# Attention with decay and a squared-ReLU layer on one core: maxima sent as rows of 32, whole heads loaded ahead and rounded on VectorE, bulk loads on another queue, the clamp on GpSimd

## The chip, the cores and the metric

The kernel runs on one core of a Trainium2 chip. A core has TensorE (PE; its weight loads are shown as PEld), VectorE (DVE), ScalarE (ACT), GpSimd (POOL) and SyncE (SP), which here only issues DMA transfers. The metric is the device time of one execution in microseconds (us), lower is better. "Granted clock" is the share of full speed at which TensorE was allowed to run.

## What is computed

Attention with a learned decay over 64 heads (8 batches of 8 heads, S = 576 tokens, D = 64), and behind it a layer of two products with a squared ReLU, all in fp32 accuracy:

```python
scores = scale * q @ k.T                                # per head, 576 x 576
cum    = cumsum(log(clip(f, 1e-4, 1)))                  # per head, 576
scores = where(causal, -1e9, scores + cum[:, None] - cum[None, :])
scores = scores - max(scores, -1)                       # the row maxima
attn   = exp(scores); attn /= sum(attn, -1) + 1e-9
x      = (attn @ v), heads side by side                 # 4608 x 512
out    = relu(x @ w_in) ** 2 @ w_out                    # 512 -> 2048 -> 512
```

## The kernel before

**Heads.** Each head is worked in 6 units (the slots of the program); unit u of head h is slot 6h+u. A unit multiplies a tile of keys with a range of queries into a PSUM bank (`score`), ACT takes the exponential (L370), and two slots later the result is multiplied with v (`av_part`). The decay and the row maxima are not added by another instruction: they are additional rows under q and k, so that the same product contains them. Row D+2 of the q plane holds minus the maximum of each query's row, so no unit of a head can begin before that row is complete.

**Maxima.** While head h-1 is worked, TensorE computes rounded scores of head h (`max_units`, L320), DVE reduces each of 6 pieces (L326) to a column `tcol` of 128 (or 64) partitions, one column for each of 5 query tiles. As soon as a column is complete, SP sends it by DMA into row D+2 of the q plane (L332), five transfers a head.

**Two kinds of heads.** Heads 0 to 13 are "whole": the scores are fp32 products of the unrounded planes `rl` (L353), for which q and k are loaded twice, once rounded on the way (`load_rounded`, a DMA on POOL's queue into `rk`, L261) for the maxima and once as they are (`load_whole`, on SP's queue). Two buffers each. Heads 14 to 63 are split into rounded and remainder parts (L360, L363, L396 to L398).

**Weights.** The 32 weight arrays of 512 KB (`w0` to `w31`, 16 each of w_in and w_out) are loaded on SP's queue and split into a rounded and a remainder part by `weight_ops`, a generator that yields five times per weight: the clamp of the magnitudes (DVE, L201); the shift (DVE, L206) with the absolute value of the next weight (ACT, L190); two combining operations (DVE, L211 and L213; behind the second the next loads are issued, four weights ahead); the rounding (ACT, L218) with the subtraction (POOL, L219). `RATES` says how many yields are taken per slot: 1 up to slot -7, 2 in slots -6 to -1, 1.2 in slots 0 to 47, 2.5 from there. The layer behind the attention (`mlp1`, L483, and `mlp2`, L506) fills TensorE from slot 60 on, when the first batch's attention is finished; from then on half-steps of it are spread over the slots.

**Order.** TensorE, ACT, DVE and POOL execute in the order in which the program is traced. SP's order is set by a scheduler. The transfers that SP and ACT issue share 8 completion semaphores (DMAHW0 to DMAHW7) in turn; before a transfer is issued, its issuing queue waits until the earlier one with that semaphore has landed. SP and POOL issue all transfers of the kernel before.

## Time and profile before

| what | value |
|---|---|
| median of 3 executions | 1244.87 us (1244.57 to 1246.03) |
| the profiled execution | 1246.64 us |
| its span, first to last instruction | 1244.9 us |
| mean granted clock | 0.980 |
| TensorE busy | 1184.0 us (95%) |
| DVE, ACT, POOL busy | 787.3, 702.7, 372.1 us |
| all DMA | 71.91 MB, 58 GB/s on average |

The span is cut into stages below: the start (up to the first units), the whole heads, the beginning of the layer, and the long stretch from 300 us in which TensorE works almost without a break. Busy shares over the whole span say little of the first two stages.

### The profile page before, as it was taken

What the parts mean: (1) busy time and instruction counts of PE and PEld (TensorE: products, weight loads), DVE (VectorE), ACT (ScalarE), POOL (GpSimd) and SP (SyncE); (2) the same over time, 40 slices, a digit from 0 to 9 for tenths busy, and PEclk for the clock granted to TensorE, in tenths of its full rate; (3) what the DMA queues carried; (4) which work ended last, traced back from release to release, by engine and by line L of the source; (5) the groups of instructions that cost most, each with busy time, mean ns of one, the idle gap of its engine ahead of it and who ended that gap; (6) DMA issues with size and microseconds to landing.
All of it is one profiled execution on the core that took longest, in us unless ns stands there. A gap on an engine that the chain in (4) does not pass through costs nothing. (4 is left out here: it accounts for less than half of the span.)

```text
span 1244.9 us, 23235 instructions
## 1 busy us (share of the span) xinstructions
PE 1184.0 (95%) x7652; PEld 1045.4 (84%) x7652; DVE 787.3 (63%) x2044; ACT 702.7 (56%) x1720; POOL 372.1 (30%) x564
## 2 busy tenths in 40 slices
PE   3887899999999999999999999999999999999998
PEld 1554677888999899999999989998998899999997
DVE  6667777666677667666656666667666767533332
ACT  3564454665666666665565556766666666632332
POOL 3233323333333333332322233334333333200000
PEclk9888799999999999999999999999999999999999
DMA  8776641112121212121212121212121222000000
GB/s 186 170 164 162 161 124 27 42 41 57 37 53 36 48 41 58 41 58 26 52 22 53 31 53 35 54 35 55 41 58 41 57 41 53 16 28 1 18 18 17
DMA packets 115640, 71.91 MB, mean 58 GB/s; under 512 B 97384, under 2 KB 97384, under 8 KB 115520
## 3 DMA queue, kind: packets, MB, share of 16 engines
q1 hardware_dynamic: 114400, 66.30, 21.9%
q0 software_dynamic: 1120, 4.13, 1.6%
q8 instruction: 61, 1.00, 0.3%
q14 instruction: 59, 0.48, 0.1%
HBM read 60.20 MB, written 9.88 MB: 56 GB/s over the span
## 5 line engine op out<-in xcount | busy, mean ns | idle before, releaser
L506 PE MATMUL bank<-w,gh 128*128 128x512 f32 x1152 | 413.2, 399 | 0.0
L483 PE MATMUL bank<-xh,w 128*128 128x256 f32 x2304 | 330.0, 286 | 3.5 <-DVE tcol L326 3.4
L386 DVE TENSOR_TENSOR pl<-p,ph 128x320 fp32r<-128x320 f32 (+4 forms) x300 | 187.7, 626 | 199.4 <-ACT ph L385 195.1
L483 PEld LDWEIGHTS bank<-xh,w 128*128 128x128 f32 x2304 | 302.0, 190 | 11.5 <-DVE tcol L326 4.0
L506 PEld LDWEIGHTS bank<-w,gh 128*128 128x128 f32 x1152 | 217.1, 188 | 38.4
L506 PE MATMUL bank<-w,gl 128*128 128x512 f32 x576 | 226.8, 394 | 0.1
L491 ACT ACTIVATE r<-bank 128x256 f32<-128x256 f32 x288 | 110.6, 384 | 205.5 <-PE bank L483 180.5
L492 DVE TENSOR_TENSOR g<-r 128x256 f32<-128x256 f32 x288 | 126.3, 439 | 140.6 <-ACT r L491 139.8
L372 POOL TENSOR_SCALAR_AFFINE_SELECT p<-p 128x128 f32<-128x128 f32 (+1 forms) x250 | 80.9, 324 | 440.3 <-ACT p L370 335.5
L385 ACT CAST ph<-p 128x320 fp32r<-128x320 f32 (+4 forms) x300 | 124.4, 415 | 148.3 <-POOL p L372 105.9
L483 PE MATMUL bank<-xl,w 128*128 128x256 f32 x1152 | 185.0, 283 | 0.0
L326 DVE CUSTOM_DVE_ANT_0 bank<-bank,mz 128x256 f32<-128x256 f32 (+4 forms) x320 | 133.7, 433 | 47.8 <-PE bank L320 43.0
L483 PEld LDWEIGHTS bank<-xl,w 128*128 128x128 f32 x1152 | 158.7, 191 | 0.0
L370 ACT ACTIVATE p<-bank 128x320 f32<-128x320 f32 (+4 forms) x300 | 116.2, 388 | 65.5 <-PE bank L363 54.2
L494 DVE TENSOR_TENSOR gl<-g,gh 128x256 fp32r<-128x256 f32 x288 | 128.3, 446 | 35.4 <-PE bank L506 0.5
L320 PE MATMUL bank<-rk 66*128 66x320 f32 (+4 forms) x384 | 114.9, 328 | 25.8 <-DMA rk<-qkraw 16.1
L493 ACT ACTIVATE gh<-r 128x256 fp32r<-128x256 f32 x288 | 120.5, 418 | 9.1
L506 PEld LDWEIGHTS bank<-w,gl 128*128 128x128 f32 x576 | 109.0, 189 | 14.2 <-DVE gl L494 0.9
L320 PEld LDWEIGHTS bank<-rk 66*128 66x128 f32 (+1 forms) x384 | 70.5, 190 | 43.4 <-issue 18.6
L396 PE MATMUL bank<-pl,vh 128*65 128x320 f32 (+4 forms) x350 | 97.2, 278 | 2.2 <-ACT den L432 2.2
L397 PE MATMUL bank<-ph,v 128*64 128x320 f32 (+4 forms) x350 | 94.9, 271 | 0.0
L398 PE MATMUL bank<-ph,vh 128*65 128x320 f32 (+4 forms) x350 | 93.6, 273 | 0.0
(76 smaller groups left out, 1512.9 us busy)
## 6 DMA issues: line engine op xcount, KB each, us to landing
qkraw<-in_qk SPq DMA_DIRECT2D x50, 288.0 KB
v<-in_v SPq DMA_DIRECT2D x64, 160.0 KB
den<-rdr SPq DMA_DIRECT2D x64, 144.0 KB
out<-osb SPq DMA_DIRECT2D x36, 256.0 KB
w<-in_w_in SPq DMA_DIRECT2D x16, 512.0 KB
w<-in_w_out SPq DMA_DIRECT2D x16, 512.0 KB
rl<-in_qk SPq DMA_DIRECT2D x14, 288.0 KB
rk<-in_qk POOLq DMA_DIRECT2D x14, 288.0 KB, 4.9
```

Of the source, the lines that this page charges most:

```text
L320: nc.tensor.matmul(ps[:m, :n], st["r2"][:D + 2, q0:q0 + m], st["kl0"][:D + 2, k0:k0 + n], start=True, stop=True,)
L326: nc.vector.tensor_tensor_reduce(out=ps[:m, :n], in0=ps[:m, :n], in1=mz[:m, mo:mo + n], op0=ALU.add, op1=ALU.min, scale=-1.0, scalar=init, ...
L370: nc.scalar.activation(out=p[:kn, :n], in_=ps[:kn, :n], func=AF.Exp, scale=SCALE)
L385: nc.scalar.copy(out=ph[:kn, :n], in_=p[:kn, :n])
L386: nc.vector.tensor_tensor(out=pl[:kn, :n], in0=p[:kn, :n], in1=ph[:kn, :n].bitcast(F32), op=ALU.subtract,)
L396: nc.tensor.matmul(acc[:D + 1, o], vh, pl[:kn, i], start=first, stop=False)
L483: nc.tensor.matmul(ph[:, :T], w[:, s, cc], x[:, cc, :], start=(cc == 0 and k == 0), stop=(cc == NCC - 1 and k == 2),)
L491: nc.scalar.activation(out=r, in_=ph[:, :T], func=AF.Relu)
L492: nc.vector.tensor_tensor(out=g, in0=r, in1=r, op=ALU.mult)
L493: nc.scalar.activation(out=gh, in_=r, func=AF.Square)
L494: nc.vector.tensor_tensor(out=gl, in0=g, in1=gh.bitcast(F32), op=ALU.subtract)
L506: nc.tensor.matmul(po, g[:, ts], w[:, s], start=(fc == 0 and k == 0), stop=(fc == NF - 1 and k == 2),)
```

## The change

- The columns of maxima stay on chip until a head's last one is there. `tcol` is cleared first; one DVE transpose of 32x32 blocks turns it into `row`, where a partition holds 32 maxima of a query tile; six transfers on SP's queue (four of 4x32 elements, two of 32) write row D+2. `row` has one buffer.
- The rounding DMA on POOL's queue is gone. Each whole head is loaded once, into one of three buffers (the third shares the memory of `qkraw`), two to three heads ahead, and two DVE copies a head (`round_whole`) make the rounded planes for the maxima.
- The weights, the v of the whole heads and the q/k of whole heads from head 2 on are issued by ACT's queue and no longer by SP's.
- The clamp of the magnitudes is on POOL.
- `RATES` is (0, 2, 1.4, 2.5). With it only w0's load is issued ahead of slot -6.
- 52 products of a zero tile are put ahead of and between the maxima of head 0 (`spin`); nobody reads their bank.

```diff
     whole = [planes(wk, F32, "rl") for _ in range(2)]
+    NWB = 3
...
+    def third_whole():
+        whole.append(planes(wk, F32, "qkraw"))
+        constant_rows(nc.gpsimd, whole[2])
...
-                nc.sync.dma_start(out=raw, in_=(w_in, w_out)[i % 2][i // 2].bitcast(I32))
+                nc.scalar.dma_start(out=raw, in_=(w_in, w_out)[i % 2][i // 2].bitcast(I32))
...
         stage()
+        yield
         stage()
-        yield
         magnitude(0)
         yield
...
-            nc.vector.tensor_scalar(mag, mag, MAG_LOW, MAG_HIGH, ALU.max, ALU.min)
+            nc.gpsimd.tensor_scalar(mag, mag, MAG_LOW, MAG_HIGH, ALU.max, ALU.min)
...
-    def load_rounded(h):
+    def load_whole(h):
         x = rounded[h % 2]
-        state[h] = dict(r2=x.q, kl0=x.k, p={})
-        nc.gpsimd.dma_start(out=x.raw[:D], in_=qk[h])
+        state[h] = dict(r2=x.q, kl0=x.k, whole=whole[h % NWB], p={})
+        x = state[h]["whole"]
+        (nc.scalar if h > 1 else nc.sync).dma_start(out=x.raw[:D], in_=qk[h])
         if cum:
             load_cum(h, x.k)
-    def load_whole(h):
-        x = state[h]["whole"] = whole[h % 2]
-        nc.sync.dma_start(out=x.raw[:D], in_=qk[h])
+    def round_whole(h):
+        x, r = state[h]["whole"], rounded[h % 2]
+        nc.vector.tensor_copy(out=r.q[:D], in_=x.q[:D])
+        nc.vector.tensor_copy(out=r.k[:D, :S], in_=x.k[:D, :S])
         if cum:
-            load_cum(h, x.k)
+            load_cum(h, r.k)
...
-            nc.sync.dma_start(out=vr[:, :, :D], in_=v[h])
+            (nc.scalar if h < NWHOLE else nc.sync).dma_start(out=vr[:, :, :D], in_=v[h])
...
         tcol = wk.tile([P, 8], F32, name="tcol")
+        nc.vector.memset(tcol, 0.0)
...
-            if last:
+            if i == 0:
                 r = st["whole"].q if h < NWHOLE else st["r2"].bitcast(F32)
-                nc.sync.dma_start(out=r[D + 2:D + 3, q0:end], in_=acc)
+                row = wk.tile([P, 32], F32, name="row", bufs=1)
+                nc.vector.transpose(
+                    out=row.rearrange("p (a c) -> p a c", c=8),
+                    in_=tcol.rearrange("p (a c) -> p a c", a=1).broadcast_to([P, 4, 8]),
+                )
+                for b in range(P // 32):
+                    nc.sync.dma_start(
+                        out=r[D + 2:D + 3, D + b * 32:D + NI * P].rearrange("o (c x) -> o c x", x=32)[:, ::P // 32],
+                        in_=row[b * 32 + 1:b * 32 + 1 + NI],
+                    )
+                for b in range(D // 32):
+                    nc.sync.dma_start(out=r[D + 2:D + 3, b * 32:(b + 1) * 32], in_=row[b * 32:b * 32 + 1])
...
-    RATES = (1, 2, 1.2, 2.5)
+    RATES = (0, 2, 1.4, 2.5)
...
-                at((h - 3) * NU + 3, 0, load_rounded, h)
-                at((h - 2) * NU + 5, 1, load_whole, h)
+            if h > 2:
+                at((h - 3) * NU + 5, 1, load_whole, h)
+            if h > 1:
+                at((h - 2) * NU + 3, 0, round_whole, h)
...
+    spun = psum.tile([P, 512], F32, name="bank7")
+    def spin(n):
+        for _ in range(n):
+            nc.tensor.matmul(spun[:, :MW], mz[:, :P], mz, start=True, stop=True)
+    for i, x in enumerate(MAXIMA[False]):
+        at(int(x) - NU, int(2 * x) % 2, spin, 2 if i < 5 else 14)
+    spin(28)
     load_f()
-    load_rounded(0)
+    load_whole(0)
     convert(1)
-    load_whole(0)
     decay()
...
-    load_rounded(1)
     load_whole(1)
+    round_whole(1)
+    third_whole()
+    load_whole(2)
```

The order of the instructions moves with it, on three engines. In the rows below `w0` to `w6` are the weights, `wmag` the magnitudes, `osb` the combined words, `ph` and `pl` the exponentials; what stands in brackets are the semaphores that an instruction waits for (DMAHW: a transfer's, with the name of an engine: that engine's).

ACT before, from the first magnitude to the first exponential of head 0:

```order
L190 ACTIVATE wmag_129<-w0_100 128x512 [waits DMAHW1_49]
L190 ACTIVATE wmag_134<-w1_102 128x512 [waits DMAHW2_49,DVE_49]
L218 CAST w0_144<-osb_132 128x512 [waits DVE_49,Activation_49]
L190 ACTIVATE wmag_158<-w2_138 128x512 [waits DMAHW4_49,DVE_49]
L218 CAST w1_176<-osb_156 128x512 [waits DVE_49,Activation_49]
L190 ACTIVATE wmag_191<-w3_140 128x512 [waits DMAHW6_49,DVE_49]
L218 CAST w2_197<-osb_189 128x512 [waits DVE_49,Activation_49]
L190 ACTIVATE wmag_203<-w4_142 128x512 [waits DMAHW7_49,DVE_49]
L370 ACTIVATE ph_207<-bank1_205 128x320 [waits PE_49]
```

The same piece of ACT's order in the changed kernel (`qkraw` is the third buffer, here for head 2):

```order
L269 DMA qkraw_158<-in_qk 64x1152 [waits DMAHW4_49,DMAHW5_49,DMAHW3_49,DMAHW6_49,DMAHW2_49,DMAHW7_49,DMAHW0_49,DVE_49]
L187 DMA w1_172<-in_w_out 128x1024
L196 ACTIVATE wmag_189<-w1_172 128x512 [waits DMAHW5_49,DVE_49]
L187 DMA w2_203<-in_w_in 128x1024
L187 DMA w3_205<-in_w_out 128x1024 [waits DMAHW1_49]
L187 DMA w4_207<-in_w_in 128x1024
L284 DMA v_209<-in_v 128x5x64 [waits DMAHW1_49]
L224 CAST w0_237<-osb_187 128x512 [waits DVE_49,Activation_49]
L196 ACTIVATE wmag_243<-w2_203 128x512 [waits DMAHW7_49,DVE_49]
L187 DMA w5_247<-in_w_out 128x1024 [waits DMAHW2_49]
L224 CAST w1_249<-osb_241 128x512 [waits DVE_49,Activation_49]
L391 ACTIVATE ph_255<-bank1_253 128x320 [waits PE_49]
```

The loads now stand in ACT's own row of work: one magnitude and two roundings stand behind the loads of w2 to w4 and v, and the first exponential behind all of them. DMAHW1 in the row of v is the semaphore of w3.

POOL in the changed kernel, the first weights:

```order
L207 TENSOR_SCALAR wmag_174<-wmag_174 128x512 [waits Activation_49,Pool_49]
L286 MEMSET v_209 128x5x2
L225 TENSOR_TENSOR w0_237<-osb_187,w0_237 128x512 [waits Activation_49]
L207 TENSOR_SCALAR wmag_189<-wmag_189 128x512 [waits Pool_49]
L225 TENSOR_TENSOR w1_249<-osb_241,w1_249 128x512 [waits DMAHW5_49,Activation_49]
L207 TENSOR_SCALAR wmag_243<-wmag_243 128x512 [waits Pool_49]
L286 MEMSET v_294 128x5x2
L225 TENSOR_TENSOR w2_308<-osb_265,w2_308 128x512 [waits DMAHW7_49,Activation_49]
```

Before, POOL had only the subtractions (L219) here, with the rounding loads between them. Now the clamp of the next weight stands behind the subtraction of this one.

SP around the maxima of a split head, before:

```order
L447 DMA rdr_4229<-cmp_4148 128x9 [waits DMAHW7_49,DMAHW2_49,DVE_49]
L246 DMA qkraw_4278<-in_qk 64x1152 [waits DMAHW3_49,Activation_49,Pool_49]
L332 DMA rk_1_77<-tcol_4163 1x128x1 [waits DMAHW4_49,DVE_49]
L332 DMA rk_1_77<-tcol_4163 1x128x1 [waits DMAHW5_49,DVE_49]
L450 DMA den_3852<-rdr_4229 64x576 [waits DMAHW6_49,DMAHW2_49]
L332 DMA rk_1_77<-tcol_4163 1x64x1 [waits DVE_49]
L450 DMA den_3852<-rdr_4229 64x576 [waits DMAHW0_49]
L255 DMA rk_0_76<-cum_dr_82 2x576 [waits DMAHW1_49,PE_49]
```

and in the changed kernel:

```order
L468 DMA rdr_4879<-cmp_4799 128x9 [waits DMAHW6_49,DMAHW5_49,DVE_49]
L253 DMA qkraw_4933<-in_qk 64x1152 [waits DMAHW7_49,Activation_49,Pool_49]
L471 DMA den_4511<-rdr_4879 64x576 [waits DMAHW6_49,DMAHW0_49]
L471 DMA den_4511<-rdr_4879 64x576 [waits DMAHW1_49]
L348 DMA rk_1_77<-row_4925 1x4x32 [waits DMAHW2_49,DVE_49]
L348 DMA rk_1_77<-row_4925 1x4x32 [waits DMAHW3_49]
L348 DMA rk_1_77<-row_4925 1x4x32 [waits DMAHW4_49]
L348 DMA rk_1_77<-row_4925 1x4x32
L353 DMA rk_1_77<-row_4925 1x16x2
L353 DMA rk_1_77<-row_4925 1x16x2 [waits DMAHW7_49]
L262 DMA rk_0_76<-cum_dr_82 2x576 [waits DMAHW0_49,PE_49]
```

Single columns stood between the two transfers of `den` (the reciprocal row sums of the heads before); now all six rows stand behind both.

More of the change, by code (lines that the diff above doesn't have):

```diff
@@ L116, in planes @@
     def planes(pool, dtype, name):
[L117 removed]
+        return Planes(pool.tile([P, S + SK], dtype, name=name, **(dict(bufs=1) if name == "qkraw" else {})))
     rounded = [planes(cpool, F32R, f"rk_{i}") for i in range(2)]
     whole = [planes(wk, F32, "rl") for _ in range(2)]
+    NWB = 3
     vhs = [cpool.tile([P, NJ, D + 2], F32R, name=f"vh_{i}") for i in range(2)]
@@ L146, in decay @@
         ft, zt, ct = (fr[:NH, i, :] for i in range(3))
+        constant_rows(nc.vector, rounded[0])
         nc.vector.memset(zt, 0.0)
-        constant_rows(nc.vector, rounded[0])
         nc.vector.tensor_scalar(ft, ft, 1e-4, 1.0, ALU.max, ALU.min)
@@ L153, in decay @@
         nc.scalar.activation(out=warm_exp[:, :1], in_=warm_exp[:, :1], func=AF.Exp)
+        round_whole(0)
         nc.vector.tensor_tensor_scan(ct, zt, ft, 0.0, ALU.add, ALU.add)
@@ L239, in decay_attention_relu2_kernel @@
     NU = len(UNITS)
+    NI = len(QT) - 1
     state = {}
@@ L438, in finish @@
         if part == 0:
-            st["cmp"] = wk.tile([P, S // D], F32, name="cmp")
+            st["cmp"] = wk.tile([P, S // D], F32, name="cmp", bufs=1)
             for i in range(2):
```

1 line of the change is left out of this document (removed).

## The prediction

> **What bounds the kernel now.** I read first where the time is, in the page's slices and in a table by stage, then in the stages that are not full what TensorE waits for.
>
> ```profile
> PE   3887899999999999999999999999999999999998
> PEclk9888799999999999999999999999999999999999
> 0.00:34.00 34.00, 12.34 (x40) 7.95 (x41) 22.42 (x54) 11.92 (x20) 12.78 (x32) 1.00 0.84 188
> 34.00:131.00 97.00, 76.58 (x331) 49.12 (x330) 65.49 (x177) 51.59 (x120) 31.20 (x37) 0.82 0.70 164
> 131.00:300.00 169.00, 157.50 (x980) 134.87 (x979) 120.50 (x281) 93.09 (x227) 53.39 (x66) 0.96 0.28 72
> 300.00:1075.00 775.00, 771.28 (x5243) 703.19 (x5243) 522.35 (x1405) 489.23 (x1214) 271.80 (x424) 1.00 0.19 45
> ```
>
> The last four rows give a stretch, its length, then the busy time of PE, PEld, DVE, ACT and POOL, the granted clock, the DMA share and GB/s. From 300 us on PE is busy in 771 of 775 us at full clock: the change removes no product there, so it can only lose there. What can be gained lies ahead of 131 us, in the whole heads, where PE is busy 79% of the time at a granted 0.82. There the first unit of each head waits for its row of maxima:
>
> ```profile
> PE bank L353 <- DMA rl<-tcol: 9.3, 5, 2.9
> 24.71 0.87 PE L353 MATMUL bank<-rl 67*128 67x320 f32 x1 [4.32 <-DMA w<-in_w_out]
> 33.40 0.49 PE L353 MATMUL bank<-rl 67*128 67x320 f32 x1
> 42.24 0.51 PE L353 MATMUL bank<-rl 67*128 67x320 f32 x1 [1.18 <-DMA rl<-tcol]
> 49.54 0.28 PE L417 MATMUL bank<-pl,v 66*65 66x64 f32 x2
> 52.58 0.87 PE L353 MATMUL bank<-rl 67*128 67x320 f32 x1 [2.76 <-DMA rl<-tcol]
> 63.81 0.49 PE L353 MATMUL bank<-rl 67*128 67x320 f32 x1
> 106.23 0.87 PE L353 MATMUL bank<-rl 67*128 67x320 f32 x1 [4.71 <-issue]
> 117.76 0.51 PE L353 MATMUL bank<-rl 67*128 67x320 f32 x1
> 131.20 0.85 PE L353 MATMUL bank<-rl 67*128 67x320 f32 x1
> ```
>
> These are the first products of heads 0, 1, 2, 3, 4, 8, 9 and 10 (49.54: the last of head 2). Head 2 takes 7.6 us of PE (42.24 to 49.82) at full speed; head 3, begun behind an idle time of 2.76 us with a product of 0.87 us in place of 0.51, takes 11.2. Heads 1 to 7 take 72.8 us, 10.4 each; heads 8 and 9 take 11.5 and 13.4. All that follows is counted from these starts, since the layer begins with head 10 and fills PE from there.
>
> **The start of head 0: +9.** Today ACT has the loads of nobody in its order, and the first exponential comes 0.18 us after the product:
>
> ```profile
> 26.15 0.44 ACT L370 ACTIVATE ph<-bank 128x320 f32<-128x320 f32 x1 [0.18 <-PE bank L353]
> 16.80 0.32 SPq L255 DMA_DIRECT2D rk<-cum_dr  x1
> 11.50 1.26 POOL L219 TENSOR_TENSOR w<-osb,w 128x512 fp32r<-128x512 f32 x1 [3.78 <-issue]
> 10.74 0.62 ACT L218 CAST w<-osb 128x512 fp32r<-128x512 f32 x1 [0.83 <-DVE osb L213]
> 8.78 0.43 DVE L206 TENSOR_SCALAR osb<-wmag 128x512 int32<-128x512 int32 x1
> 9.96 0.69 DVE L213 SCALAR_TENSOR_TENSOR osb<-w,osb 128x512 int32<-128x512 int32 x1
> 2.31 0.57 POOL L132 MEMSET rl<- 32x576 f32 x1
> ```
>
> In the change ACT first issues head 2's q/k into the memory that held the cumulated sums, so it waits until those are stored; they are first read back at 16.80, which I take. Then w1 goes out, about 17.4. At 188 GB/s (first stage) 288 and 512 KB need 1.6 and 2.8 us: w1 is there at about 21.5, its magnitude follows, and w2 to w4 go out by 23. The load of v waits for the semaphore of w3, which is 5.6 us of transfers later, about 28. Behind it stand w0's rounding (0.62, 28.9) and, by way of POOL's subtraction (1.26) and the clamp of w1, DVE's shift (0.43) and two combinations (0.69 each), the rounding of w1 (0.62). No row shows the clamp on POOL; it lies between POOL's memset (0.57, one operand fewer) and its subtraction of two operands (1.26). I take the middle, 0.95. That gives 31.1, 32.9, 33.5 and the first exponential at about 34, 8 us later than now. PE fills its three banks at 25 and then waits, so it begins anew at half speed, as head 3 shows: about 1 us more. Bounds: -5, if fewer bytes let the first product come earlier than 24.71 (it waited 4.32 us) and nothing of the above binds, to +12.
>
> Of the zero products, which run in PE's idle time ahead of 24.71, nothing is left after so long a wait: 0. The Trainium skill ("TensorE: Matmul & The Clock Gate", Part 1, "What's actually happening") has an idle window of about 3.4 us after which the clock falls again; head 3's 2.76 us on this trace were enough already.
>
> **Heads 1 to 7: -7.** Three chains compete with the 7.6 us of PE. First the row of maxima:
>
> ```profile
> 47.95 0.14 DVE L326 DVE_READ_ACCUMULATOR2_ANT tcol<- 64x1 f32 x1
> 67.90 1.19 SPq L442 DMA_DIRECT2D cmp<-den  x2
> 70.48 0.18 DVE L444 TENSOR_SCALAR cmp<-cmp 128x9 f32<-128x9 f32 x1 [0.26 <-DMA cmp<-den]
> 17.23 0.23 SPq L255 DMA_DIRECT2D rl<-cum_dr  x1
> 340.16 0.39 SPq L255 DMA_DIRECT2D rk<-cum_dr  x1
> 338.84 0.59 SPq L332 DMA_DIRECT2D rk<-tcol  x1
> ```
>
> The last maximum of head 3 is read 5.85 us after head 2's start (48.09) and PE gets its row 4.5 us later. Now come a transpose (0.2, from the small operation at 70.48), four issues, and the landing of the last (from 69.09 to 70.4: 1.3). An issue of few pieces took 0.23 to 0.39 (L255, two rows), one of 128 pieces 0.59 (L332); the rows have four pieces, so 0.36 each, 1.45 in all. Sum 2.95, so a head takes at least 8.8; with other transfers in the way up to the present 4.5, 10.4.
>
> Second, the weights. Today the clamp on DVE does not wait for POOL. In the change clamp, shift, two combinations, rounding and subtraction of a weight follow each other, and the next clamp stands behind the subtraction on POOL: 0.95 + 0.43 + 0.69 + 0.69 + 0.62 + 1.26 = 4.64, and five handovers of about 0.1: 5.1 a weight. At 1.4 yields a slot a head has 1.68 weights: 8.6 us. Third, DVE and ACT lose the clamps and gain two roundings of 64x576 a head; 65 and 52 of 97 us leave room. I take 9.4, between the row's 8.8 and the 10.4 of now: 7 times -1.0. Bounds: 7.6 (-19.6) to 10.9 (+3.5).
>
> **Heads 8 and 9: +5.** At 2.5 yields a slot there are three weights a head. Now they follow at 3.5 us:
>
> ```profile
> 118.93 1.48 POOL L219 TENSOR_TENSOR w<-osb,w 128x512 fp32r<-128x512 f32 x1 [2.02 <-ACT w L218]
> 122.46 1.27 POOL L219 TENSOR_TENSOR w<-osb,w 128x512 fp32r<-128x512 f32 x1 [2.06 <-ACT w L218]
> 127.49 1.26 POOL L219 TENSOR_TENSOR w<-osb,w 128x512 fp32r<-128x512 f32 x1 [3.76 <-ACT w L218]
> 127.60 1.48 DVE L206 TENSOR_SCALAR osb<-wmag 128x512 int32<-128x512 int32 x1
> ```
>
> With 5.1 each they need 15.3 a head, against 11.5 and 13.4: +5.7; some of it can run over into head 10, so +5. Bounds -3 to +8. The shift of 1.48 us at 127.60 in place of 0.43 shows DVE slowed while POOL subtracts. The Trainium skill ("SBUF — State Buffer", section "SBUF: two separate sides") has a port pair shared by POOL and DVE, which one of them holds for a whole instruction while the other is blocked; this row agrees. By that rule the clamp on POOL, in place of one on DVE, stops DVE more often, for up to 0.95 us each time: with 1.68 clamps a head and seven heads at most 11 us, if DVE had no room.
>
> **Heads 10 to 18: 0.** They have 19 to 25 us each and 93% of PE; the clamps of the last 10 weights find room. Bounds -4 to +4.
>
> **Split heads: +6.** Here the row has no gain to make, only a margin to lose:
>
> ```profile
> 337.92 0.13 DVE L326 DVE_READ_ACCUMULATOR2_ANT tcol<- 64x1 f32 x1
> 341.72 0.31 PE L360 MATMUL bank<-rk 67*128 67x320 f32 x1
> 422.32 0.13 DVE L326 DVE_READ_ACCUMULATOR2_ANT tcol<- 64x1 f32 x1
> 424.37 0.31 PE L360 MATMUL bank<-rk 67*128 67x320 f32 x1
> 338.24 0.55 SPq L450 DMA_DIRECT2D den<-rdr  x1
> ```
>
> From the last maximum to the head's first product there are 3.67 us in most heads, and 1.92 in the shortest; in about ten of fifty (heads 18, 22, 26, 30, 42, 46 and so on) it is 1.8 to 3.1, 2.4 on average. The row needs 2.95, so these ten wait 0.55 each. The two `den` transfers (0.55 each) that now stand ahead of the rows cost nothing as long as they go before the last maximum; the columns that held them up are gone. If they do not, 1.1 us are added in every second head. Bounds 0 to +45 (issues of 0.59 and `den` in front).
>
> **The sum.** 9 - 7 + 5 + 0 + 6 = +13 on the profiled 1246.64 gives 1259.6. That execution lies 1.8 above the median of the runs, so I forecast **1258**. By bounds alone it could go from -32 to +73.
>
> **Rivals.** *Faster:* ACT's queue does not hold the start, because its transfers land sooner and the clamp is near 0.57, and the heads come down to the row's chain with a fast landing: start +2, heads 1 to 7 at 8.4 (-14), heads 8 and 9 -2: about 1231. For it speaks that PE is idle for 20 of the 97 us of the whole heads, at a granted 0.82, and that each whole head's q/k is loaded once instead of twice, at a DMA share of 0.84 and 0.70; against it the order of ACT, in which a wait for a transfer stops roundings and exponentials. The Trainium skill ("DMA: Bandwidth & Descriptors", section "Issuing engines are not separate DMA queues") holds that another issuing queue brings no bandwidth, only issue time; by it the move to ACT has nothing to give but the time of SP, and this rival rests on the saved bytes alone. *No change:* start and heads 8 and 9 (+14) are made good by heads 1 to 7 near 8.6 (-13): 1245 to 1247. *Rows late everywhere, slower by more:* issues take 0.5 and the `den` pair goes first: 0.2 + 2.0 + 1.3 + 1.1 = 4.6 against 3.67 in every second head, about 25 x 0.9, and 1.1 in ten others, 33 in all; with the +7 of the early stage 1285, or 1269 if it holds in half of them. It decides from an issue of 0.54 on without `den`, of 0.27 with both in front.
>
> **How the numbers follow.** My forecast 0.42, with its own range 1248 to 1270; faster 0.30; no change 0.12; rows late 0.16. Within 0.2% (2.5 us) is what a measurement of this kernel cannot tell from no change: 0.12; faster 0.30; slower 0.58. The range for 8 in 10 takes in the faster rival's 1231 and most of the late rows: 1229 to 1278.
>
> **What would show it.** Right: first exponential near 34, head 1 near 42; heads 1 to 7 at 9 to 10 us; subtractions of weights 5 us apart in heads 8 and 9 with POOL's clamp between them near 0.95; a PE wait on the row DMA in about ten split heads. Wrong: a first exponential before 29, a head 8 that begins before 100, or a wait on the rows in more than half of the split heads.

## The result: 6.7% slower

The changed kernel takes 1328.43 us (median of 4 executions, 1326.14 to 1331.02); the kernel before, timed beside it, 1245.45 us. The ratio is 1.0666 (95% interval 1.0641 to 1.0692): +83 us where +13 was forecast, and outside the range.

The table by stage, cut at the first products of heads 1, 10, 18 and 63. First the kernel before (columns as in the prediction: stretch, length, busy time of PE, PEld, DVE, ACT and POOL, granted clock, DMA share, GB/s):

```profile
0.00:33.40 33.40, 11.73 (x38) 7.55 (x38) 21.86 (x53) 11.32 (x19) 12.78 (x32) 1.00 0.84 189
33.40:131.20 97.80, 77.38 (x337) 49.70 (x335) 66.26 (x178) 52.19 (x121) 31.27 (x37) 0.82 0.70 165
131.20:292.53 161.33, 150.18 (x928) 128.14 (x927) 115.57 (x269) 86.29 (x211) 51.32 (x62) 0.96 0.29 74
292.53:1073.81 781.28, 777.20 (x5285) 708.55 (x5284) 525.88 (x1416) 494.92 (x1229) 272.74 (x427) 1.00 0.19 45
```

The changed kernel:

```profile
0.00:44.23 44.23, 26.89 (x90) 13.17 (x90) 18.14 (x53) 9.50 (x16) 18.42 (x35) 0.73 0.41 121
44.23:176.68 132.45, 101.42 (x335) 63.41 (x335) 67.07 (x204) 53.33 (x123) 60.21 (x48) 0.63 0.39 109
176.68:351.23 174.55, 154.31 (x926) 129.08 (x926) 116.07 (x279) 87.48 (x213) 69.63 (x72) 0.94 0.22 59
351.23:1157.27 806.04, 783.97 (x5283) 705.80 (x5284) 540.16 (x1504) 495.09 (x1226) 270.66 (x427) 1.00 0.17 43
```

Every stage is longer: +10.8 up to head 1, +34.7 in heads 1 to 9, +13.2 in heads 10 to 17, +24.8 in heads 18 to 62, together the 83.4 us between the spans (1244.9 and 1328.3). From the first product of head 63 on, both take 171 us. The DMA share fell from 0.70 to 0.39 in heads 1 to 9, as each of them is loaded once, and that bought nothing. The granted clock there fell from 0.82 to 0.63, and TensorE's busy time rose from 77.4 to 101.4 us with the same products (337 and 335 records): 24 of the 34.7 us are slower products, 10.6 are more idle time.

TensorE's waits name two things, the rows of maxima and the maxima themselves (line, what it waited for: us in total, times, longest):

```profile
PE bank L381 <- DMA rk<-row: 23.7, 29, 2.3
PE bank L330 <- DVE tcol L336: 17.9, 14, 5.2
PE bank L374 <- DMA rl<-row: 17.8, 6, 3.9
PE bank L504 <- DVE tcol L336: 6.3, 1, 6.3
PE bank L374 <- DMA qkraw<-row: 6.3, 2, 3.5
```

**The rows.** In the time lines of DVE, SP, ACT and PE around the last maximum before head 3, and around one split head, head 25:

```profile
67.31 0.13 DVE L336 DVE_READ_ACCUMULATOR2_ANT tcol<- 64x1 f32 x1
67.48 0.21 DVE L343 STREAM_TRANSPOSE row<-tcol 128x32 f32<-128x32 f32 x1
67.72 0.65 SPq L348 DMA_DIRECT2D rl<-row  x1
68.45 0.52 SPq L463 DMA_DIRECT2D cmp<-den  x1
69.03 1.89 SPq L348 DMA_DIRECT2D rl<-row  x3
69.45 0.34 ACTq L187 DMA_DIRECT2D w<-in_w_in  x1
73.63 0.87 PE L374 MATMUL bank<-rl 67*128 67x320 f32 x1 [3.73 <-DMA rl<-row]
...
465.19 0.14 DVE L336 DVE_READ_ACCUMULATOR2_ANT tcol<- 64x1 f32 x1
465.60 2.57 SPq L348 DMA_DIRECT2D rk<-row  x4
468.21 1.18 SPq L353 DMA_DIRECT2D rk<-row  x2
469.34 0.39 PE L381 MATMUL bank<-rk 67*128 67x320 f32 x1 [0.19 <-DMA rk<-row]
```

A head's first product reads queries 256 to 575 and so needs four of the six transfers. In the split head these four issues take 2.57 us, 0.64 each, and the product begins 1.2 us after the last of them: 4.0 us from the last maximum, a little over the usual margin of 3.67. Before head 3 the same work takes 6.2 us. A transfer of the row sums (L463) stands between the first row and the others, and the product comes 2.7 us after the fourth; a weight's load (512 KB) was issued by ACT meanwhile, at 69.45. TensorE stands for 3.73 us and begins again at half clock (0.87 us for a product in place of 0.51).

**The clamp.** The groups of instructions of the changed kernel for clamp, subtraction and shift (busy time, mean ns of one; idle time of the engine before them and what ended it):

```profile
L207 POOL TENSOR_SCALAR wmag<-wmag 128x512 f32<-128x512 f32 x32 | 62.8, 1963 | 0.7 <-ACT wmag L196 0.7
L225 POOL TENSOR_TENSOR w<-osb,w 128x512 fp32r<-128x512 f32 x32 | 41.6, 1300 | 130.3 <-ACT w L224 116.4 <-DMA w<-in_w_in 7.9 <-DMA rl<-in_qk 6.0
L212 DVE TENSOR_SCALAR osb<-wmag 128x512 int32<-128x512 int32 x32 | 19.1, 597 | 65.2 <-POOL wmag L207 49.1 <-POOL v L286 16.1
```

The shift in the kernel before:

```profile
L206 DVE TENSOR_SCALAR osb<-wmag 128x512 int32<-128x512 int32 x32 | 22.5, 704 | 2.5
```

The clamp takes 1.96 us on POOL, twice the estimate. DVE stands idle for 65 us ahead of its 32 shifts, waiting for POOL (49 us for the clamp, 16 for the small fill of `v` that stands behind some of the clamps); in the kernel before the same group had 2.5 us. Since DVE works in the traced order, the maxima stand behind the shift and wait with it.

### The profile page after: what moved, and what is told of

Its sections match the earlier page's. It is cut to its first block, busy times and chain, and to the rows that moved or that the text cites. A ratio compares the mean times of both kernels' runs of the same rounds, so it can differ in the third digit from the quotient of the medians.

```text
span 1328.3 us, 23358 instructions
## 1 busy us (share of the span) xinstructions
PE 1234.0 (93%) x7704; PEld 1062.9 (80%) x7704; DVE 798.4 (60%) x2168; ACT 703.1 (53%) x1720; POOL 422.1 (32%) x586
## 4 chain that ended last, share of the span: by engine, by line
PE 47%; DVE 4%; DMA 4%; SPq 4%; issue 2%; ACT 1%; POOL 0%; DVEq 0%; ACTq 0%; POOLq 0%
PE bank L504 19%; PE bank L527 17%; SPq L348 4%; DMA rk<-row 3%; PE bank L417 2%; PE bank L381 2%; PE bank L330 2%; PE bank L419 2%; PE bank L418 2%; PE bank L384 1%; DVE g L513 1%; DVE pl L407 1%; DVE bank L336 1%; ACT r L512 1%; DVE gl L515 1%
## 5 line engine op out<-in xcount | busy, mean ns | idle before, releaser
L407 DVE TENSOR_TENSOR pl<-p,ph 128x320 fp32r<-128x320 f32 (+4 forms) x300 | 196.7, 656 | 214.3 <-ACT ph L406 205.3
L513 DVE TENSOR_TENSOR g<-r 128x256 f32<-128x256 f32 x288 | 136.3, 473 | 139.3 <-ACT r L512 138.8
L330 PE MATMUL bank<-rk 66*128 66x320 f32 (+4 forms) x384 | 121.9, 347 | 21.3 <-DVE tcol L336 17.9
L381 PE MATMUL bank<-rk 67*128 67x320 f32 (+4 forms) x300 | 89.6, 299 | 24.8 <-DMA rk<-row 23.7
L330 PEld LDWEIGHTS bank<-rk 66*128 66x128 f32 (+1 forms) x384 | 74.1, 199 | 42.5 <-DVE tcol L336 26.9
```

The lines of the kernel that those rows point to most:

```text
L330: nc.tensor.matmul(ps[:m, :n], st["r2"][:D + 2, q0:q0 + m], st["kl0"][:D + 2, k0:k0 + n], start=True, stop=True,)
L407: nc.vector.tensor_tensor(out=pl[:kn, :n], in0=p[:kn, :n], in1=ph[:kn, :n].bitcast(F32), op=ALU.subtract,)
L513: nc.vector.tensor_tensor(out=g, in0=r, in1=r, op=ALU.mult)
```

## The experiments

Three theories: the rows make the loss (1), the clamp behind the subtraction on POOL does (2), the loads in ACT's order do (3). Each run is the changed kernel or the kernel before with one edit, and then with several. The results first, by stage; the first column of lengths ends at the first product of head 1. The ratio is taken against the kernel before as timed on the same chip. The lengths are those of one profiled execution each, which lies within 1.6 us of its kernel's median, with two exceptions here: "all three undone" was profiled 4.1 us above its median, and "the same, loads by ACT" 7.0 us below.

| kernel | to head 1 | heads 1-9 | heads 10-17 | heads 18-62 | median us | ratio to before (95%) |
|---|---|---|---|---|---|---|
| before | 33.4 | 97.8 | 161.3 | 781.3 | 1245.45 | |
| changed | 44.2 | 132.5 | 174.6 | 806.0 | 1328.43 | 1.0666 (1.0641-1.0692) |
| changed, columns | 39.7 | 121.5 | 174.2 | 779.4 | 1286.34 | 1.0330 (1.0291-1.0369) |
| changed, clamp on DVE | 36.5 | 121.2 | 163.6 | 808.9 | 1301.47 | 1.0452 (1.0411-1.0492) |
| changed, loads by SP | 39.1 | 122.3 | 174.1 | 809.5 | 1318.33 | 1.0587 (1.0556-1.0618) |
| changed, more zero products | 46.5 | 119.1 | 176.2 | 805.8 | 1320.75 | 1.0606 (1.0576-1.0637) |
| before, with rows | 34.9 | 117.0 | 168.6 | 808.1 | 1301.57 | 1.0451 (1.0410-1.0492) |
| before, with clamp on POOL | 35.5 | 113.2 | 186.6 | 780.1 | 1286.98 | 1.0334 (1.0292-1.0376) |
| all three undone | 31.2 | 103.4 | 158.1 | 780.5 | 1242.64 | 0.9984 (0.9962-1.0006) |
| the same, loads by ACT | 34.3 | 95.4 | 158.3 | 780.0 | 1248.21 | 1.0028 (1.0004-1.0052) |
| clamp on DVE, rows by SP and ACT | 39.6 | 114.5 | 171.5 | 867.3 | 1366.42 | 1.0972 (1.0917-1.1028) |
| changed, clamp earlier on POOL | 37.8 | 118.7 | 161.0 | 808.3 | 1300.09 | 1.0440 (1.0387-1.0492) |

### Columns again in the changed kernel

```diff
-        nc.vector.memset(tcol, 0.0)
...
-            if i == 0:
-                row = ...; transpose; six transfers
+            if last:
                 r = st["whole"].q if h < NWHOLE else st["r2"].bitcast(F32)
+                nc.sync.dma_start(out=r[D + 2:D + 3, q0:end], in_=acc)
```

> The changed kernel with one part undone: each column of maxima goes out by its own transfer when it is ready, as before; loads, clamp, buffers, zero products stay. Theory 1 (the rows carry the loss: six issues of 0.6 us on SP behind the last maximum make 5.8 us to the next head's first product, where it was 4.5, and the idle time holds the clock at half): the whole heads fall from 13 to 15 us to about 11, head 10 begins near 145 instead of 176.7, the split heads are back at 16.2 us (-25), time about 1270. Theory 2 (the clamp on POOL, 1.92 us, holds DVE's shift and with it maxima and exponentials): only the split heads' 25 us come back, head 10 stays near 172, time about 1300. Theory 3 (ACT's queue): as theory 2.

Measured: 1286.34 us. The split heads give back the whole of their 25 us (779.4), as all three theories had it. Heads 1 to 9 give back only 11 us; between the 145 of theory 1 and the 172 of theory 2, head 10 begins at 161.2. TensorE's largest wait is now the maxima on DVE, whose shifts still stand idle for 67.9 us behind POOL:

```profile
PE bank L329 <- DVE tcol L335: 25.3, 18, 4.9
PE bank L426 <- ACT ph L379: 8.9, 6, 3.5
```

### The clamp on DVE in the changed kernel

```diff
-            nc.gpsimd.tensor_scalar(mag, mag, MAG_LOW, MAG_HIGH, ALU.max, ALU.min)
+            nc.vector.tensor_scalar(mag, mag, MAG_LOW, MAG_HIGH, ALU.max, ALU.min)
```

> The changed kernel with one part undone: the clamp of the magnitudes is on DVE again. Theory 2: DVE's shift no longer waits 3 to 4 us for POOL, a weight takes about 4.5 us instead of 6 to 7, head 10 begins near 150 and heads 10 to 17 lose their 13 us: time about 1290. Theory 1: the rows still hold each head at 13 us at half clock, head 10 begins at 168 or later; time 1315 to 1320. Either way the split heads, where no weight is converted, keep their 25 us.

Measured: 1301.47 us; head 10 begins at 157.7, again between the two theories (150 and 168). Heads 10 to 17 give back 11 of their 13 us, where the columns gave nothing back (174.2), so in the changed kernel that loss is the clamp's. Heads 1 to 9 give back 11 of 35; there the wait on the rows holds them now (25.0 us in 11 waits), where it was the maxima with the columns. The two parts cover one another: each undone alone gives 11 us in heads 1 to 9.

### Loads by SP, and zero products ahead of the heads

```diff
-                nc.scalar.dma_start(out=raw, in_=(w_in, w_out)[i % 2][i // 2].bitcast(I32))
+                nc.sync.dma_start(out=raw, in_=(w_in, w_out)[i % 2][i // 2].bitcast(I32))
...
-        (nc.scalar if h > 1 else nc.sync).dma_start(out=x.raw[:D], in_=qk[h])
+        nc.sync.dma_start(out=x.raw[:D], in_=qk[h])
...
-            (nc.scalar if h < NWHOLE else nc.sync).dma_start(out=vr[:, :, :D], in_=v[h])
+            nc.sync.dma_start(out=vr[:, :, :D], in_=v[h])
```

> The changed kernel with one part undone: weights, v and q/k of the whole heads are issued by SP again. Theory 3 (loads in ACT's order hold exponentials and roundings behind a transfer's landing): first exponential at about 27 instead of 33.8, head 10 near 165, time about 1315. Against it: SP gets some 25 issues of 0.5 us more among the rows in the whole heads, so rows come later still; if that weighs more, time 1330 to 1345. The split heads do not change.

Measured: 1318.33 us, near the 1315 of theory 3. Five us come back at the start and ten in heads 1 to 9; the split heads take 3.5 us more. ACT's queue has a part in the loss, the smallest of the three. Before head 3, where the changed kernel had the late product shown above, the lines are now:

```profile
60.13 2.57 SPq L348 DMA_DIRECT2D rl<-row  x4
63.98 0.51 PE L374 MATMUL bank<-rl 67*128 67x320 f32 x1 [2.24 <-DMA rl<-row]
```

The product comes 1.28 us after the fourth row's issue, not 2.7, and in all of heads 1 to 10 it comes 1.09 to 1.28 us after it. In the changed kernel the heads among these that wait for a row have 1.1 to 2.7. So the late landings go with bulk loads that are issued beside the rows.

```diff
             h, u = slots[n]
+            if u == 0 and 0 < h < 10:
+                spin(10)
             score(h, u)
```

> The changed kernel with ten more products of the zero tile ahead of the first product of heads 1 to 9 (1.9 us of TensorE at full clock, 3.7 at half), so that the idle time there is filled. If the half clock is what stretches the whole heads (granted 0.63 from 44 to 177 us), they go from 14 to about 11.5 us, head 10 begins near 155 and the time is about 1306. If the chain of weights and maxima on DVE, POOL and SP sets them, and the clock only follows, head 10 stays within 4 us of 176.7 and the time within 1322 to 1334.

Measured: 1320.75 us, between the two. The granted clock from head 1 to head 10 goes from 0.63 to 0.86, and those heads from 132.5 to 119.1 us. The start is 2.3 us longer and heads 10 to 17 are 1.7 us longer, so that 8 us of the time come back. So the half clock is worth some 13 us of the 35 in heads 1 to 9, perhaps more, since the zero products take time themselves; 21 us are left at a clock above that of the kernel before (0.82), and these must be the chains of the rows and the weights.

### One part at a time on the kernel before

> The kernel before with one part of the change: the maxima leave as rows of 32 (and one buffer for the reciprocal sums, which makes room). The chain from the last maximum to the next head's first product is 5.8 us in place of 4.5 and holds on every whole head; SP also has the weights' loads in its order here. Head 10 begins 10 to 20 us later than 131.2, the split heads lose 25 us as in the changed kernel: 1275 to 1290. If the rows were harmful only together with ACT's loads and POOL's clamp, the whole heads stay and the time is about 1270; if they cost nothing in this order of SP, 1245.

> The kernel before with one part of the change: the clamp of the magnitudes on POOL. If the clamp (1.92 us, behind the subtraction and ahead of the shift) holds DVE and ACT by itself, head 10 begins 15 to 20 us later than 131.2, heads 10 to 17 lose about 12 more, the split heads nothing: 1270 to 1280. If it hurts only where the rows already make the heads long, less than 10 us: below 1255.

```diff
 (rows: the changed kernel's lines from "if i == 0" on, the cleared tcol, and)
-            st["cmp"] = wk.tile([P, S // D], F32, name="cmp")
+            st["cmp"] = wk.tile([P, S // D], F32, name="cmp", bufs=1)
 (clamp:)
-            nc.vector.tensor_scalar(mag, mag, MAG_LOW, MAG_HIGH, ALU.max, ALU.min)
+            nc.gpsimd.tensor_scalar(mag, mag, MAG_LOW, MAG_HIGH, ALU.max, ALU.min)
```

Measured: 1301.57 and 1286.98 us, both slower than expected. Rows alone cost 19 us in heads 1 to 9, 7 in heads 10 to 17 and 27 in the split heads. The clamp alone costs 15 in heads 1 to 9 and 25 in heads 10 to 17, and nothing where no weight is converted. Each needs no other part of the change to do harm. They harm in different places: in heads 1 to 7 the rows cost 16.4 us and the clamp 5.2, in heads 8 and 9, with three weights a head, the rows 2.8 and the clamp 10.3. Their costs in heads 1 to 9, 19 and 15, add up to the 35 of the changed kernel; in heads 10 to 17 the changed kernel loses less (13) than the clamp does alone, and in the whole time the two alone lose 57 and 43 us, the changed kernel 83.

### What is left without the three

```diff
 (columns, clamp on DVE, loads by SP as above; kept: three buffers and one load of a
  whole head, rounding by DVE, RATES, zero products)
```

> The changed kernel with three parts undone (columns, clamp on DVE, loads issued by SP). What is left of the change: each whole head loaded once into three buffers and rounded by DVE, the pace of the weights, the zero products. If the three losses add up (42, 27 and 10 us of the 83), this is at 1245 to 1250. If each of them alone keeps the heads long, so that undoing them together gives more, the smaller number of bytes shows: 1230 to 1242. If what is left costs something of its own (maxima that wait for roundings, weights that begin later), 1255 or more.

> The same with the loads issued by ACT, as in the change (columns, clamp on DVE). With the two waits on POOL and the rows gone, ACT's queue costs at most its late first exponential: 5 to 10 us more than the kernel with SP's loads of the same call. If its transfers hold up exponentials in every head, 15 or more. If it costs nothing or gains, the loss in the changed kernel was that its late start met the slow weights.

Measured: 1242.64 us, ratio 0.9984 (0.9962 to 1.0006), no difference from the kernel before that can be told; and with the loads by ACT 1248.21 us, 1.0028 (1.0004 to 1.0052). What is kept, the saved loads among it, gives no more than a few us; ACT's queue costs some 5 us (its interval lies just above 1), half of what it cost in the changed kernel. Against this second kernel, whose heads 1 to 9 take 95.4 us in the execution profiled, the rows alone add 25.8 us there (the kernel with the clamp on DVE), the clamp alone 26.1 (the kernel with columns), both 37.1. That execution was 7 us faster than the median, so the three figures may each be some us too high; but by the ratios too the rows add 4.2% of the time before, the clamp 3.0% and both 6.4%, less than their sum. That a head which waits for its clamp has its rows' wait partly behind it would explain this; it was not shown by itself.

### Why the rows are late: two queues for them

```diff
                 for b in range(P // 32):
-                    nc.sync.dma_start(
+                    (nc.sync, nc.scalar)[b % 2].dma_start(
...
                 for b in range(D // 32):
-                    nc.sync.dma_start(
+                    (nc.sync, nc.scalar)[b % 2].dma_start(
```

> The changed kernel with the clamp on DVE (as in the run at 1301) and one more edit: of the six row transfers of a head, every second one is issued by ACT. If the serial issues on SP (0.57 to 0.67 us each) make the row late, three in place of six save 1.9 us: the stretch from head 18 to head 63 goes from 809 us to 781 to 788, head 10 from 157.7 to about 145, time about 1262 to 1275. If the landing (1.0 us alone, 3 us behind a 512 KB load) is what counts, the split heads keep more than 800 us and the time stays above 1293. If ACT, which then waits for the transpose with exponentials behind it, loses more than SP gains: above 1301.

This is the kernel with the clamp on DVE and one more edit. Measured: 1366.42 us, the third case. The wait on the rows falls, as the serial issues would have it, but ACT pays for it. The first three rows are TensorE's waits, the last two ACT's time line in a split head:

```profile
PE bank L504 <- ACT r L512: 49.8, 44, 1.6
PE bank L438 <- ACT pl L391: 19.7, 10, 4.5
PE bank L381 <- DMA rk<-row: 8.4, 10, 1.3
...
507.47 1.24 ACTq L348 DMA_DIRECT2D rk<-row  x2
509.40 0.57 ACT L406 CAST ph<-p 128x448 fp32r<-128x448 f32 x1 [2.51 <-DMA rk<-row]
```

The waits of the split heads on rows fall from 22.7 us (30 times) in the kernel with the clamp on DVE to 8.4 (10 times). ACT, which reaches its three transfers in traced order before the transpose is done, stands for 2.51 us with a rounding behind them, and TensorE waits for it in the layer. The longer heads of this kernel (867 us in place of 809) would shorten the wait on a row by themselves, so the wait alone proves little. The row's chain proves it: in the ten heads with the shortest margin, the first product comes 3.06 to 3.19 us after the last maximum, and with all six transfers on SP it came after 3.93 to 4.55. So the serial issues make the rows late, though two queues save 0.9 us there and not the 1.9 that were expected.

### Why the clamp hurts: its place, not its length

```diff
             if i < NW:
                 mags[i] = wk.tile([P, DM], F32, name="wmag", bufs=1)
                 nc.scalar.activation(out=mags[i], in_=words(i)[1].bitcast(F32), func=AF.Abs)
+                nc.gpsimd.tensor_scalar(mags[i], mags[i], MAG_LOW, MAG_HIGH, ALU.max, ALU.min)
...
-            nc.gpsimd.tensor_scalar(mag, mag, MAG_LOW, MAG_HIGH, ALU.max, ALU.min)
```

> The changed kernel with the clamp still on POOL, but at another place in the order: right behind ACT's magnitude, so ahead of the subtraction of the weight before and not behind it. If the order makes the loss (the shift of a weight waits for the rounding and subtraction of the one before), most of what the clamp on DVE gave comes back: head 10 near 160 instead of 176.7, heads 10 to 17 near 165 us instead of 174.6, time 1303 to 1312. If the duration of 1.92 us and POOL's share of the port with DVE make it, at most a third: 1320 to 1330.

Measured: 1300.09 us, as with the clamp on DVE (1301.47). The groups of this kernel:

```profile
L197 POOL TENSOR_SCALAR wmag<-wmag 128x512 f32<-128x512 f32 x32 | 66.3, 2072 | 54.0 <-ACT wmag L196 54.0
L212 DVE TENSOR_SCALAR osb<-wmag 128x512 int32<-128x512 int32 x32 | 18.3, 571 | 1.7 <-POOL wmag L197 1.6
```

The clamp is as long as ever (2.07 us), and DVE's wait ahead of the shifts is gone: 1.7 us instead of 65.2. One line's place on POOL, behind the subtraction or ahead of it, is worth 28 us. Theory 2 holds in this form: not POOL's speed, nor a port that it shares with DVE, but the chain clamp, shift, combinations, rounding, subtraction, clamp.

### What holds the whole heads when the losses are gone

All of these build on the kernel with the three parts undone and loads by SP (the last with loads by ACT): the first with more zero products, the others with none, and each "and" an edit on top of that. "No zero products" was profiled 4.8 us above its median and the early clamp 4.5 above, the others within 0.8, so differences of a few us between the stages of these two and the others say nothing.

| kernel | to head 1 | heads 1-9 | heads 10-17 | heads 18-62 | median us | ratio to before (95%) |
|---|---|---|---|---|---|---|
| eight zero products ahead of heads 1 to 9 | 32.9 | 100.3 | 159.1 | 779.5 | 1244.32 | 0.9998 (0.9975-1.0020) |
| no zero products | 33.1 | 99.0 | 161.6 | 780.0 | 1241.71 | 0.9986 (0.9963-1.0008) |
| and the early clamp on POOL | 34.7 | 104.0 | 158.5 | 780.1 | 1245.66 | 0.9995 (0.9971-1.0019) |
| and cumulated sums copied | 33.8 | 95.2 | 160.1 | 780.2 | 1241.72 | 0.9956 (0.9941-0.9971) |
| both | 34.7 | 98.1 | 158.6 | 779.4 | 1243.45 | 0.9981 (0.9963-1.0000) |
| both, loads by ACT | 36.7 | 95.3 | 160.1 | 779.8 | 1245.29 | 0.9987 (0.9968-1.0006) |

```diff
+            if u == 0 and 0 < h < 10:
+                spin(8)
 (and, in the other kernel)
-    for i, x in enumerate(MAXIMA[False]):
-        at(int(x) - NU, int(2 * x) % 2, spin, 2 if i < 5 else 14)
-    spin(28)
```

> The kernel with columns, clamp on DVE and loads by SP (1242.6), and eight zero products ahead of the first product of heads 1 to 9. In the changed kernel ten of them brought head 10 forward by 11 us. If the half clock costs here too (heads of 12 to 14.6 us beside heads of 6.7 to 9), head 10 goes from 134.6 to 120 to 126 and the time to 1229 to 1236, faster than the kernel before. If DVE, with the maxima behind the weights, sets the heads, head 10 stays within 4 us and the time within 1238 to 1247.

> The same kernel without the 52 zero products ahead of and in the maxima of head 0. The prediction gave them no effect. Without them head 0's maxima run at half clock: head 0 begins at about 25.5 instead of 24.5 and head 1 at 33 to 34 instead of 31.2, time 1243 to 1246. If they cost as much as they give: 1240 to 1243.

Filling the idle time with zero products lifts the granted clock (0.91 against 0.75 between 31 and 130 us) but not the time, and leaving out the 52 of the change changes nothing in the time that can be told. Head 0 did not begin later without them, as had been expected (25.5), but earlier: at 21.98, against 24.48 with them. Without the rows and the clamp, the clock follows the chains and does not set them.

The two edits for what was open are the early clamp, as above, and

```diff
-        nc.vector.tensor_copy(out=r.k[:D, :S], in_=x.k[:D, :S])
-        if cum:
-            load_cum(h, r.k)
+        n = D + 2 if cum else D
+        nc.vector.tensor_copy(out=r.k[:n, :S], in_=x.k[:n, :S])
```

> Columns, loads by SP, no zero products, and the clamp on POOL, but ahead of the subtraction. What is open: with the three losses undone the whole heads still take 10 us and more, though each is loaded once. If DVE, where the maxima stand behind the weights' operations, holds them (TensorE's waits for maxima are 11 us there), the clamps taken off DVE bring head 10 from 132 to 126 to 129 and the time to 1234 to 1239. If DVE is not what holds them, or POOL's clamp slows DVE through the port, 1241 to 1248.

> Columns, loads by SP, no zero products, clamp on DVE; and the two rows of cumulated sums of the rounded plane are copied by DVE together with k (66 rows in place of 64) and no longer loaded by a transfer of their own behind the other loads of SP. If the waits of the maxima for that transfer (8 to 10 us in the whole heads) hold the heads, head 10 comes at 124 to 128 and the time is 1233 to 1238. If another wait takes their place, as the rows took the clamp's, 1239 to 1245.

> Both edits together. If DVE and the late rows are two chains side by side, of which the one holds when the other is gone, both together give more than the sum of the two: head 10 at 118 to 124, 1226 to 1233. If the columns' transfer behind the last maximum is the limit (4.5 us), 1234 to 1242.

> The same as the one with both edits, with the loads issued by ACT as in the change. If a load in ACT's order holds exponentials only while something else is late, this is within 3 us of it; if ACT's queue has a price of its own, 5 to 10 us slower; if SP's columns gain from a queue without bulk loads, 3 to 8 us faster.

All four miss what would have been a gain. Taking the clamps off DVE gives nothing: TensorE waits 12.3 us for the maxima, and 12.5 without the edit. Copying the cumulated sums takes their wait away (3.8 us without the edit); the time, 1241.72 us, is in the band that was expected for another wait in its place, and no shorter than without the edit (1241.71). The wait in its place is the columns' transfer (4.9 us without the edit), beside that for DVE, in the rows of this kernel:

```profile
PE bank L328 <- DVE tcol L334: 14.2, 14, 5.6
PE bank L361 <- DMA rl<-tcol: 9.6, 5, 3.3
PE bank L361 <- DMA qkraw<-tcol: 2.5, 1, 2.5
```

With both edits nothing is added: 1243.45 us lies above both cases that were expected. With ACT's queue it is the same within 2 us. The kernel with copied sums is the only one whose interval lies below that of the kernel before, by 0.44% (0.29 to 0.59%); but its median is that of the kernel without the edit, which was timed beside a kernel before of 1244.3 us where this one stood beside 1246.25, so that the gain can't be put down to the edit. What would bring the whole heads to the 7.6 us of TensorE's work was not found.

## Why the prediction was wrong, point by point

- **The direction, and where it can only be lost: right.** The split heads lost, and the largest single loss lies ahead of head 10.
- **The start, +9: right in size (+10.8), in part by luck.** The first exponential was forecast for 34 and came at 33.80, behind w1's rounding as described:

```profile
33.80 0.43 ACT L391 ACTIVATE ph<-bank 128x320 f32<-128x320 f32 x1
29.35 0.51 PE L374 MATMUL bank<-rl 67*128 67x320 f32 x1 [3.15 <-DMA rl<-row]
```

  Two errors met there: v's load was issued at 26.73 and not at 28, and the clamp took 1.0 us longer than its estimate. Not foreseen is that head 0's first product is late itself (29.35, not 24.71), waiting for its rows. And the queue alone does not hold the exponential: with columns and the clamp on DVE but the loads by ACT, it comes at 26.23 (26.15 in the kernel before). With one part undone it comes at 28.30 (clamp on DVE), 28.52 (loads by SP) or 29.24 (columns), so most of the delay needs all three together.
- **Heads 1 to 7, -7: the step that failed, in sign too.** They took 97.3 us, +24.5. The prediction divided a head in two: 5.85 us from its first product to the last maximum of the next head, taken as fixed, and from there the row's chain, which was to fall to 2.95. In the kernel before, the two parts are 6.43 and 3.97 us on average over these heads (the 5.85 was one head; they go from 5.51 to 8.95). In the changed kernel they are 9.05 and 4.85. So 18.3 of the 24.5 us lie in the part that the prediction held fixed, and 6.2 in the one that was to become shorter.

  In the row's chain two sizes were wrong. The issue of a transfer was taken as 0.36 from a transfer of two pieces (L255); it measured 0.57 to 0.67, near the 0.59 of the column transfers (L332), which was the other end of the bound. The landing, taken as 1.3, was 2.7 before head 3. In the weights' chain the clamp, taken as 0.95 in the middle of its bounds, is 1.96, above both of them.

  The larger fault is in the way the chains were put together: "side by side", the longest counts, and the first part of a head depends on none of them. But DVE and ACT take instructions in traced order, so the maxima stand behind a shift that waits for POOL, and the rows behind the maxima; and the idle time makes products slower. Of the six idle times of 3.0 to 3.9 us ahead of the first products of heads 0 to 10, five were followed by a product of 0.87 us in place of 0.51; shorter ones went either way, in the kernel before too (2.76 us and 0.87 before head 3, 2.95 us and 0.51 before head 5). Each part of the change lengthens the first part of a head by itself: on the kernel before, rows make it 7.91 us and the clamp 7.72. How much of that is the clock and how much the waits of DVE stays open. Had only the sizes been wrong, the longest chain would have been 5.85 + 4.85 = 10.7 us a head (an estimate from these rows), and a head took 13.9. On the kernel before, the costs of rows and clamp add up in heads 1 to 9; on the other base they do not. What both have in common is that the two together cost more than the dearer one alone. The bound of 10.9 us a head was taken from a single chain.
- **Heads 8 and 9, +5: right in kind, half in size.** +10.1, and the clamp alone makes +10.3 there on the kernel before. The 5.1 us a weight would have been 6.1 with the clamp's true length; the subtractions of these heads are 6.0 to 6.3 us apart. The 3.5 us that were read as the pace before are the shortest of five distances (3.5 to 5.0); the forecast did not use them.
- **Heads 10 to 17, 0 within 4: wrong.** +13.2. That the cost of the clamps would find room there was taken from busy shares; the chain of a weight is a matter of waits. With the clamp on DVE or ahead of the subtraction these heads are back at 164 and 161 us.
- **Split heads, +6: mechanism right, size wrong.** +24.8. It is the issue again: 0.27 us from the last maximum to the first issue, 2.57 for the four and 1.17 to the product make 4.0 against a margin of 3.67. So 29 of the 50 split heads wait for a row, which the prediction had named as a sign of being wrong: the ten short ones 0.6 to 2.3 us, 1.6 on average and not 0.55, most of the others 0.1 to 0.9. These waits, 23.7 us, are nearly the whole loss of the stage. The rival of late rows had put its point at an issue of 0.54 without the `den` pair; the measured 0.64 lies above it, and its 33 us for this stage were nearer than 6.
- **The gain from one load instead of two** lay under the -7 and in the faster rival. With the three parts undone, the rest of the change gives at most a few us (0.9984); the saved load was not tried by itself. The DMA share of 0.70 was not the bound. The waits that were named in the whole heads are chains of single instructions; bulk loads come in only where a row lands late beside one.
- **The zero products, 0: right.** Without them 1241.71, with them 1242.64.
- **What the prediction cited.** The Trainium skill ("DMA: Bandwidth & Descriptors", section "Issuing engines are not separate DMA queues") holds that another issuing queue gives no bandwidth, only issue time. Three pairs of kernels that differ in the queue alone agree: none gains by ACT's (SP first, 1242.64 and 1248.21, 1243.45 and 1245.29, 1318.33 and 1328.43). The port pair of POOL and DVE (the Trainium skill, "SBUF — State Buffer", section "SBUF: two separate sides") is locked by the one that starts first, on DVE's side only for some kinds of operation. The prediction drew from it up to 11 us for the clamp on POOL, wherever it stands; placed earlier, the clamp there costs no time against the one on DVE (1300.09 and 1301.47).
- **The chances:** slower had 0.58, but the upper end of the range, 1278, was taken from the late rows alone. No case had late rows and a slow weight chain together in every stage, though the sum of the worst bounds (+73) stood in the text, and even that is less than the measured +83.

## What to carry to other kernels

Where engines take instructions in traced order, look for the loop that an edit closes between them: an operation moved to an engine behind the last step of the previous round makes rounds serial, and its place in that engine's order can be worth far more than its length. A chain that runs once per head behind the last result is paid in full; count its issues one by one at the duration of the nearest transfer of the same kind, and take the dearer one. Ask of every term that a sum holds fixed what the edit will make of it. When two delays are both able to hold a stage, undo both before judging either, and do not bound the stage by one alone.

## What was not expected of the hardware

- The clamp (two scalar operations on 128x512 floats) takes 1.96 us on POOL against 0.59 on DVE, and more than POOL's subtraction of two tensors of that size (1.30 us).
- A transfer of four pieces of 128 bytes costs SP no less to issue than one of 128 pieces of 4 bytes (0.64 us on average in the split head above, 0.59 in the one of the kernel before), while one of two pieces of 2304 bytes costs 0.23 to 0.39. Fewer pieces did not mean a cheaper issue.
- The product that waits for the rows begins 1.2 us after the fourth issue in the split head shown, but 2.7 us after it before head 3, where ACT issued a load of 512 KB among the rows. With the bulk loads on SP's queue it is 1.09 to 1.28 us in all of heads 1 to 10. It is not ACT's queue as such: with the rows on the kernel before, where SP and POOL issue the loads, it is up to 3.9 us (head 8, with three loads issued in the 1.4 us ahead of the rows). That the small transfers wait behind the bytes of the large ones is the likely cause; no run took a single load away.
